# One fused linear-attention and two-MLP kernel: small first loads on SyncE's queue, late weights in one transfer each, and a new listed order

## The chip, the cores and the metric

The kernel runs on one core of one Trainium2 chip. The time is device time in microseconds (us) of one execution; the kernel before takes 922.84 us (median of three runs, 921.71 to 923.36). The engines are named as in the profile: PE is TensorE, PEld its weight loads, DVE VectorE, ACT ScalarE, POOL GpSimd, SP SyncE. SPq and ACTq mark the issue of a transfer (DMA) by SP or ACT.

## What is computed

Three stages, the output of one being the input of the next; q, k, v and the result are float32, the six weight matrices arrive as 64-bit floats. q is drawn eight times wider than k and v.

```python
def _attn_ref(q, k, v):                      # (4, 8, 576, 64) each
    q_s = softmax of q over its last axis; k_s = softmax of k over the sequence
    kv = np.einsum('bhsd,bhse->bhde', k_s, v)
    return np.einsum('bhsd,bhde->bhse', q_s, kv)
x = attention, as 2304 tokens x 512
x = (silu(x @ w_gate) * (x @ w_val)) @ w_out       # 512 -> 1536 -> 512
x = ((x @ w_a) * (x @ w_b)) @ w_out                # 512 -> 1536 -> 512
```

(The two softmaxes are written out in the reference, with 1e-9 added to each sum.)

## The kernel before, in words

**Number format.** A float32 product is made of three products in PE's fp32r format: each operand is split into a high part, rounded by a copy on ACT (L432, L542), and a low part, the rest, by a subtraction on DVE or POOL (L425 is the line of the helper that all two-operand additions and subtractions go through). The weights are read raw, as pairs of 32-bit words, and are brought to float32 by a chain of six operations on ACT, DVE and POOL (L516 to L543 for the early ones, L586 to L605 for the late ones; `a<-wr`, `early<-early` and `late<-late` in the rows).

**Attention** is cut into 16 units, one for each batch and pair of heads. The 576 rows of a head are 512 main rows, four to a partition, and a rest of 64. A unit loads k, q and v (`ut`, `ua`, `uc`, `uq`), takes the column maxima of k (`tm`, then a transposition `kx` on PE, then a reduction `kr` on DVE, L778, and a transposition back, `kb`), subtracts, exponentiates on ACT (L812 for k and q at once), multiplies k by v (`kv`, L840), scales, turns q (`qt`, `ql`) and multiplies (`xt`, `xl`). For batch 0 the rests of all four units are loaded together into one buffer `rests` by six transfers of 64 KB: two for k, two for q, two for v (`load_rests`, L622). They are issued by ACT.

**First MLP.** 1536 hidden columns are 12 blocks f. For each token tile of 512 rows and each f there are two up-products (`u`, 12 matmuls each), a gate (ACT L989, DVE L992), the split of the gated product into `h` (ACT L432, DVE L425), and four down-products into `acc`. The first two tiles run in this form. A bank of up-products comes free when `h` of the block before is written. While tile 0 runs, the kernel also converts the 12 weight blocks and does the attention of batch 1; while tile 1 runs, batches 2 and 3.

**Later.** From about 280 us on the tokens go in three groups (`SUPER`, L1162), in which the products of pairs of blocks are combined so that fewer matmuls are needed at the price of more additions (`p`, `q`, `o`, `temps`, `raww`, `l2w` in the rows). The weights of the second MLP are converted beside this, between 170 and 580 us, by `convert_late` (L561): 36 pieces of a third of a block each, 512 KB raw, into buffers `early` or `late`.

**The order.** Nothing is scheduled at run time. Every operation has a number; `ORDER` (L72) lists all 3,732 in the order in which they are handed out, and each engine works through its own in that order, waiting where an input or a buffer is not ready. `SECOND` (L42) lists the operations that run on their second possible engine (POOL in place of DVE, ACT in place of DVE, and so on), `PLACE` (L60) picks buffers, and `UNREAD` (L68) puts transpositions of the identity whose result nobody reads (`unread`, L1624) ahead of listed products, so many each. A transfer is issued by its engine in the same order, and the issue itself waits where an earlier transfer on the same semaphore has not landed (eight of them go round).

Of the kernel before, what the change touches and what calls it, by code (L numbers as in the profile page):

```python
# [30 lines left out]
class Plan:  # L31
# [27 lines left out]
    )  # L59
    PLACE = (  # L60
        "00102103011010010221301001112132030011031011101100000010001110112101000100110001111020101110001101121110"
        "00101110110021010011010001110010010101100101111110010010110100000011010001111011100101100100011111100101"
        "01010110010101000110110110100101101010101010110110111100101010000010000110110101101101001011101001101011"
        "00101001102130123020110311010102013020110311010102013020110311010102013010120311010101023021301021301010"
# [4 lines left out]
        29, 7, 31, 3, 69, 3, 101, 14, 105, 7, 43, 25, 88, 1, 141, 8, 115, 3, 151, 6, 124, 2, 128, 3, 648, 21, 255,  # L69
        1, 654, 8, 657, 17,  # L70
    )
    ORDER = (  # L72
# [270 lines left out]
def kernel(  # L343
# [24 lines left out]
    nc = tc.nc  # L368
    B, H, S, D = q.shape
    DM = H * D  # L370
    DFF = w_gate.shape[1]
    P = 128
# [12 lines left out]
    WC, WH = 512, 256  # L385
# [65 lines left out]
    mats = [[m.bitcast(U32) for m in ms] for ms in ((w_gate, w_val, w_out), (w_a, w_b, w_out2))]  # L451
# [109 lines left out]
    def convert_late(f, m):  # L561
# [3 lines left out]
        def r():  # L565
            return buf()[:, at:at + 1024].rearrange("p (h n t) -> p h n t", h=2, t=2)
# [1092 lines left out]
```

## Time and profile before

| | |
|---|---|
| median of 3 runs | 922.84 us |
| the profiled execution | 924.12 us |
| its span in the trace | 922.3 us |
| PE busy | 902.8 us (98%) |
| DVE busy | 706.6 us (77%) |
| ACT busy | 537.1 us (58%) |
| POOL busy | 400.0 us (43%) |
| granted TensorE clock, whole span | 1.00 |

The profiled execution is 1.3 us longer than the median. A span is counted from the start of the trace; 1.8 us of the 924.12 lie outside it. Busy time is the union of an engine's instructions, without the issue of transfers. A row of the timeline gives start and length in us, engine, line, operation, output and inputs, how many instructions were merged, and in brackets how long the engine sat idle before and what ended that.

### The profile page before, as it was taken

The page shows a single profiled execution, that of the slowest core. Times are in us where ns is not written, and L with a number is a line of the kernel's source. Part 1 is how long each engine was busy: PE and PEld are TensorE (multiplying, and loading weights), DVE is VectorE, ACT ScalarE, POOL GpSimd, SP SyncE. Part 2 cuts the span into 40 slices and gives each one's busy share as a digit, 9 for nine tenths or more (in the row PEclk, how much of TensorE's full clock was granted, in tenths as well). Part 3 has the DMA queues.
Part 4 walks back from the last instruction along what each step waited for, and adds up shares of the span by engine and source line. Part 5 has one row for each costly group of instructions (what it writes and reads, how often), then busy time and mean ns, then how long its engine had stood idle before and what let it go on. Part 6 is the DMA issues. An engine that isn't in the chain of part 4 may idle for free.

```text
span 922.3 us, 13897 instructions
## 1 busy us (share of the span) xinstructions
PE 902.8 (98%) x4851; PEld 757.4 (82%) x4851; DVE 706.6 (77%) x1148; ACT 537.1 (58%) x983; POOL 400.0 (43%) x380
## 2 busy tenths in 40 slices
PE   7899999999999999999999999999999999999998
PEld 6677777777787888888888888888788898988986
DVE  6999996689888698888868767547797586776845
ACT  4999976557765775655563556333544573553530
POOL 5322121344323453756356622254554343575720
PEclk9999999999999999999999999999999999999999
DMA  9888775588854323142433653212231220101003
GB/s 269 269 262 280 239 233 172 165 258 271 272 167 137 97 87 96 55 124 80 129 135 107 201 154 109 80 46 92 80 103 58 92 69 23 47 24 46 24 1 115
DMA packets 108302, 121.50 MB, mean 132 GB/s; under 512 B 31944, under 2 KB 84168, under 8 KB 108104
## 3 DMA queue, kind: packets, MB, share of 16 engines
q1 hardware_dynamic: 102568, 116.55, 40.3%
q10 hardware_dynamic: 5664, 4.07, 1.4%
q8 instruction: 38, 0.62, 0.3%
q14 instruction: 32, 0.26, 0.1%
HBM read 88.60 MB, written 31.98 MB: 131 GB/s over the span
## 4 chain that ended last, share of the span: by engine, by line
PE 73%; DVE 1%; issue 0%; DVEq 0%
PE p L1295 37%; PE o L1430 10%; PE q L1404 7%; PE u L970 2%; PE o L1432 2%; PE o L1439 2%; PE acc L1005 2%; PE o_a L1516 2%; PE o_b L1516 2%; PE o_d L1516 2%; PE o_a L1511 1%; PE o_b L1511 1%; PE o_d L1511 1%; PE o_e L1516 1%; PE o_e L1511 1%; DVE raww L425 0%
## 5 line engine op out<-in xcount | busy, mean ns | idle before, releaser
L1295 PE MATMUL p<-l2w,l2w 128*128 128x512 f32 x1512 | 360.7, 390 | 2.1 <-DVE temps L425 2.1
L1295 PEld LDWEIGHTS p<-l2w,l2w 128*128 128x128 f32 x1512 | 280.7, 188 | 59.4 <-DVE temps L425 2.9
L425 POOL TENSOR_TENSOR l2w<-raww,l2w 128x512 fp32r<-128x512 f32 x68 | 95.3, 1405 | 157.1 <-ACT l2w L432 157.0
L970 PE MATMUL u<-xhl,w 128*128 128x512 f32 x552 | 138.8, 399 | 2.6 <-DVE h L425 1.6
L432 ACT CAST l2w<-raww 128x512 fp32r<-128x512 f32 x144 | 87.8, 621 | 67.1 <-PE p L1295 23.3
L970 PEld LDWEIGHTS u<-xhl,w 128*128 128x128 f32 x552 | 100.8, 188 | 25.5 <-DVE h L425 1.9
L425 DVE TENSOR_TENSOR temps<-p,temps 128x512 f32<-128x512 f32 x90 | 61.7, 686 | 48.2 <-PE p L1295 47.6
L425 DVE TENSOR_TENSOR l2w<-raww,l2w 128x512 fp32r<-128x512 f32 x76 | 63.4, 840 | 25.4 <-ACT l2w L432 25.4
L1308 ACT COPY temps<-p 128x512 f32<-128x512 f32 x72 | 41.9, 588 | 58.1 <-PE p L1295 58.0
L1005 PE MATMUL acc<-h,w 128*128 128x512 f32 x288 | 74.6, 401 | 0.0
L1404 PE MATMUL q<-rest,l2w 128*128 128x256 f32 x432 | 65.5, 283 | 0.0
L1005 PEld LDWEIGHTS acc<-h,w 128*128 128x128 f32 x288 | 52.4, 188 | 11.9 <-issue 1.0
L425 DVE TENSOR_TENSOR sums<-o,sums 128x512 f32<-128x512 f32 (+1 forms) x65 | 44.0, 679 | 20.6 <-PE o L1430 14.8
L1404 PEld LDWEIGHTS q<-rest,l2w 128*128 128x128 f32 x432 | 58.3, 192 | 0.5
L1430 PE MATMUL o<-l2w,hp 128*128 128x512 f32 x165 | 55.5, 391 | 0.0
L425 POOL TENSOR_TENSOR raww<-raww 128x256 f32<-128x256 f32 (+1 forms) x32 | 36.6, 1144 | 41.9 <-DVE l2w L425 24.6
L1430 PE MATMUL o<-l2w,l2w 128*128 128x512 f32 x168 | 49.5, 389 | 0.0
L602 POOL TENSOR_TENSOR late<-late 128x512 uint32<-128x512 uint32 x15 | 20.8, 1384 | 51.2 <-DVE late L597 36.5
L1430 PEld LDWEIGHTS o<-l2w,l2w 128*128 128x128 f32 x168 | 31.5, 188 | 6.6
L1430 PEld LDWEIGHTS o<-l2w,hp 128*128 128x128 f32 x165 | 30.7, 188 | 6.9 <-DVE sums L425 0.4
L425 DVE TENSOR_TENSOR sums<-o_e,sums 128x512 f32<-128x512 f32 x36 | 23.8, 684 | 10.5 <-ACT sums L1535 5.0
L432 ACT CAST l2w<-temps 128x512 fp32r<-128x512 f32 x36 | 22.1, 620 | 15.9 <-PE o L1430 7.6
(264 smaller groups left out, 1793.5 us busy)
## 6 DMA issues: line engine op xcount, KB each, us to landing
raww<-wf SPq DMA_DIRECT2D x36, 512.0 KB, 3.9
raww<-wf SPq DMA_DIRECT2D x36, 256.0 KB, 3.4
wf<-a SPq DMA_DIRECT2D x16, 384.0 KB, 3.0
wr<-in_moe_w_gate_dram SPq DMA_DIRECT2D x22, 256.0 KB, 4.0
wr<-in_moe_w_val_dram SPq DMA_DIRECT2D x22, 256.0 KB, 3.7
wr<-in_moe_w_out_dram SPq DMA_DIRECT2D x22, 256.0 KB, 4.5
wf<-late SPq DMA_DIRECT2D x20, 256.0 KB, 2.4
wf<-early SPq DMA_DIRECT2D x16, 256.0 KB, 5.4
```

The lines of the kernel that those rows point to most:

```text
L425: engine.tensor_tensor(out=out(), in0=x(), in1=y(), op=op)
L432: add("scalar", act_us(n), lambda: nc.scalar.copy(out=hi(), in_=src()), src_keys, [hi_key])
L602: engine.tensor_tensor(out=u32(), in0=u32(), in1=r()[..., 0], op=ALU.add)
L970: nc.tensor.matmul(ps()[:, 0:n], lhsT=wv[:, c, :], rhs=x()[:, xs, c, 0:n], start=(a == 0 and c == 0), stop=(a == 2 and c == KD - 1))
L1005: nc.tensor.matmul(ps()[:, 0:n], lhsT=w()[:, 4 + ws, o * P:(o + 1) * P], rhs=h()[:, hs, 0:n], start=begin, stop=end)
L1295: nc.tensor.matmul(ps()[:, 0:width], lhsT=wv(o)[:, m, ws, c, :], rhs=ops_x[o][xs][1]().rearrange("p (c n) -> p c n", c=2)[:, c, 0:width], ...
L1308: add("scalar", act_us(n), lambda: nc.scalar.copy(out=to[1]()[:, 0:n], in_=ps()[:, 0:n]), [ps], to[0] if isinstance(to[0], list) else [to[ ...
L1404: nc.tensor.matmul(ps[m]()[:, 0:256], lhsT=wv(o)[:, m, ws, c % 2, :], rhs=rest_x[xs][1]().rearrange("p (c n) -> p c n", c=KD)[:, c, :], st ...
L1430: nc.tensor.matmul(ps(), lhsT=lhs(i, hs), rhs=outs_w[i][1]()[:, ws * 512:(ws + 1) * 512], **ends)
L1432: nc.tensor.matmul(ps()[:, 0:width], lhsT=outs_w[i][1]()[:, ws * 512 + r * P:ws * 512 + (r + 1) * P], rhs=hs2[i][t][1]()[:, hs * 512:hs * ...
L1511: nc.tensor.matmul(ps()[:, 0:width], lhsT=wu()[:, at:at + P], rhs=h()[:, hs * 512:hs * 512 + width], start=first and a == 0, stop=a == 2, ...
L1516: nc.tensor.matmul(ps()[:, r * 256:(r + 1) * 256], lhsT=h()[:, hs * 512 + (2 * g + r) * P:hs * 512 + (2 * g + r + 1) * P], rhs=wu()[:, ws ...
```

## The change

Three things.

1. `load_rests` issues its six transfers through SP's queue in place of ACT's. (The planner's label `queue="scalar"` stays; what is issued where is set by the call.)
2. `convert_late` loads a piece of `w_a` or `w_b` in one transfer of 512 KB, in place of two of 256 KB; 24 pieces are concerned. Pieces of `w_out` had one already.
3. `SECOND`, `PLACE`, `UNREAD` and `ORDER` are new lists for the same operations.

```diff
     UNREAD = (
-        29, 7, 31, 3, 69, 3, 101, 14, 105, 7, 43, 25, 88, 1, 141, 8, 115, 3, 151, 6, 124, 2, 128, 3, 648, 21, 255,
-        1, 654, 8, 657, 17,
+        29, 7, 31, 3, 69, 3, 101, 3, 105, 11, 43, 31, 88, 6, 141, 9, 115, 5, 124, 10, 128, 8, 648, 26, 654, 14, 657,
+        12,
     )
...
             if m < 2:
-                for h in range(2):
-                    nc.sync.dma_start(
-                        out=r()[:, h].rearrange("p (c n) t -> p c (n t)", n=P),
-                        in_=mats[1][m][h * DM // 2:(h + 1) * DM // 2, f * 2 * P:(f + 1) * 2 * P].rearrange(
-                            "(c p) n -> p c n", p=P))
+                nc.sync.dma_start(
+                    out=buf()[:, at:at + 1024].rearrange("p (c n) -> p c n", n=2 * P),
+                    in_=mats[1][m][:, f * 2 * P:(f + 1) * 2 * P].rearrange("(c p) n -> p c n", p=P))
...
         for h in range(HG):
-            dma(lambda h=h: nc.scalar.dma_start(
+            dma(lambda h=h: nc.sync.dma_start(
                 out=rests_kq()[rest(h), at, :, h, :] if at < 2 else rests_v()[rest(h)],
                 in_=src[b, :, SM:S, :].rearrange("(g h) s d -> h s g d", h=HG)[h]),
```

By instruction counts PE has 19 more of the unread transpositions (148 for 129) and is otherwise unchanged, SP has 18 transfers fewer (24 fewer late ones, six rests more), ACT six fewer issues, and some ten operations change between DVE, POOL and ACT. On PE the new order moves single attention products by a few places up to about 236 us and leaves everything after that as it was. Line numbers after L575 are two lower in the changed file.

**The first transfers.** On SP the kernel starts with these rows; `ut0` to `ut3` are the four units of batch 0, `wr0_0_0` is the first third of weight block 0. Before:

```order
L715 DMA ut0_92<-in_k_dram 128x2x256
L715 DMA ut1_94<-in_k_dram 128x2x256
L715 DMA ut0_92<-in_q_dram 128x2x256
L715 DMA ut1_94<-in_q_dram 128x2x256
L715 DMA ut2_105<-in_k_dram 128x2x256
L715 DMA ut2_105<-in_q_dram 128x2x256
L487 DMA wr0_0_0_123<-in_moe_w_gate_dram 128x4x256
L715 DMA ut3_125<-in_k_dram 128x2x256
L715 DMA ut3_125<-in_q_dram 128x2x256
L726 DMA ut0_92<-in_v_dram 128x4x64 x2
L726 DMA ut1_94<-in_v_dram 128x4x64 x2
```

In the changed kernel:

```order
L713 DMA ut0_92<-in_k_dram 128x2x256
L713 DMA ut1_94<-in_k_dram 128x2x256
L713 DMA ut0_92<-in_q_dram 128x2x256
L713 DMA ut1_94<-in_q_dram 128x2x256
L623 DMA rests_97<-in_k_dram 64x4x64 x2
L713 DMA ut2_103<-in_k_dram 128x2x256
L713 DMA ut2_103<-in_q_dram 128x2x256
L487 DMA wr0_0_0_126<-in_moe_w_gate_dram 128x4x256
L713 DMA ut3_128<-in_k_dram 128x2x256
L713 DMA ut3_128<-in_q_dram 128x2x256
L724 DMA ut0_92<-in_v_dram 128x4x64
L623 DMA rests_97<-in_q_dram 64x4x64 x2
L623 DMA rests_97<-in_v_dram 64x4x64 x2
L724 DMA ut0_92<-in_v_dram 128x4x64
```

The six transfers of `rests` now stand in SP's row: k behind the first four tiles, q and v behind the gate weights, k and q of unit 3 and half of v of unit 0.

On DVE the same stretch begins (the first three rows are alike) with `kr0`, the column maxima of unit 0; `st` holds the row maxima of q, and `st0<-rests` is the one that reads the rest of q. Before:

```order
L778 TENSOR_REDUCE kr0_136<-kx0_117 128x1
L778 TENSOR_REDUCE kr1_140<-kx1_132 128x1
L797 TENSOR_REDUCE st0_142<-ut0_92 128x8
L425 TENSOR_TENSOR ut0_92<-ut0_92,kb0_153 128x2x4x64
L800 TENSOR_REDUCE st0_142<-rests_97 128x1
L797 TENSOR_REDUCE st1_161<-ut1_94 128x8
L800 TENSOR_REDUCE st1_161<-rests_97 128x1
L425 TENSOR_TENSOR ut1_94<-rests_97,kb1_156 128x128
L425 TENSOR_TENSOR tm2_169<-ut2_105 128x2x2x64
```

In the changed kernel:

```order
L776 TENSOR_REDUCE kr0_132<-kx0_115 128x1
L776 TENSOR_REDUCE kr1_138<-kx1_130 128x1
L795 TENSOR_REDUCE st0_140<-ut0_92 128x8
L425 TENSOR_TENSOR tm2_160<-ut2_103 128x2x2x64
L795 TENSOR_REDUCE st1_162<-ut1_94 128x8
L798 TENSOR_REDUCE st0_140<-rests_97 128x1
L776 TENSOR_REDUCE kr2_173<-kx2_169 128x1
L425 TENSOR_TENSOR ut1_94<-rests_97,kb1_154 128x128
L425 TENSOR_TENSOR tm3_176<-ut3_128 128x2x2x64
L798 TENSOR_REDUCE st1_162<-rests_97 128x1
L425 TENSOR_TENSOR ut1_94<-ut1_94,kb1_154 128x2x4x64
```

The rest maxima of q of unit 0 stood behind a subtraction and ahead of unit 1's; now they stand ahead of `kr2`, `kb1`'s subtraction and all that follows. The subtraction `ut0<-ut0,kb0` has gone to POOL.

**Weight block 7 beside tile 0, f = 5.** On DVE, where `h0_0_5` is the low part of the gated product of block 5 and `a0_7_0`, `a0_7_1` are the two halves of weight block 7 in conversion. Before:

```order
L523 TENSOR_SCALAR a0_7_0_1136<-a0_7_0_1136 128x768
L526 TENSOR_SCALAR a0_7_0_1136<-a0_7_0_1136 128x768
L532 SCALAR_TENSOR_TENSOR a0_7_0_1136<-wr0_7_0_1062,a0_7_0_1136 128x768
L518 TENSOR_SCALAR a0_7_1_1170<-wr0_7_1_1111 128x768
L537 ISA a0_7_0_1136<-wr0_7_0_1062,a0_7_0_1136 128x1536
L523 TENSOR_SCALAR a0_7_1_1170<-a0_7_1_1170 128x768
L425 TENSOR_TENSOR h0_0_5_1189<-u0_0_5_1_1100,h0_0_5_1189 128x512
```

In the changed kernel:

```order
L523 TENSOR_SCALAR a0_7_0_1152<-a0_7_0_1152 128x768
L526 TENSOR_SCALAR a0_7_0_1152<-a0_7_0_1152 128x768
L425 TENSOR_TENSOR h0_0_5_1181<-u0_0_5_1_1117,h0_0_5_1181 128x512
L532 SCALAR_TENSOR_TENSOR a0_7_0_1152<-wr0_7_0_1076,a0_7_0_1152 128x768
L518 TENSOR_SCALAR a0_7_1_1185<-wr0_7_1_1128 128x768
L537 ISA a0_7_0_1152<-wr0_7_0_1076,a0_7_0_1152 128x1536
```

`h0_0_5` has moved ahead of the operation that reads the second half's raw words (`a0_7_1<-wr0_7_1`), and three others.

**The change from the second group of tokens to the third.** On DVE; `p11_0_1` and so on are banks of up-products of step 11, `raww` and `spare` hold float32 weights, `r12`, `r2a01` and `r2wr11` tokens. Before:

```order
L425 TENSOR_TENSOR temps_3136<-p11_0_1_6158,temps_3136 128x512
L425 TENSOR_TENSOR l2w2_2869<-r12_6168,l2w2_2869 128x1024
L425 TENSOR_TENSOR temps_3136<-p11_0_2_6150,temps_3136 128x512
L425 TENSOR_TENSOR r12_6168<-r12_6168,r2a01_6173 128x1024
L425 TENSOR_TENSOR r2a01_6173<-r2a01_6173,r2wr11_6175 128x1024
L425 TENSOR_TENSOR raww_2932<-raww_2932,spare_3022 128x512
L425 TENSOR_TENSOR temps_3136<-p11_1_1_6211,temps_3136 128x512
```

In the changed kernel:

```order
L425 TENSOR_TENSOR temps_3136<-p11_0_1_6150,temps_3136 128x512
L425 TENSOR_TENSOR raww_2936<-raww_2936,spare_3027 128x512
L425 TENSOR_TENSOR l2w2_2869<-r12_6160,l2w2_2869 128x1024
L425 TENSOR_TENSOR temps_3136<-p11_0_2_6142,temps_3136 128x512
L425 TENSOR_TENSOR r12_6160<-r12_6160,r2a01_6165 128x1024
L425 TENSOR_TENSOR r2a01_6165<-r2a01_6165,r2wr11_6167 128x1024
L425 TENSOR_TENSOR temps_3136<-p11_1_1_6204,temps_3136 128x512
```

The subtraction `raww<-raww,spare` has moved from right ahead of `temps<-p11_1_1,temps` to five places earlier.

## Rows read from the trace of the kernel before

**Rows 1.** Windows: stretch, its length, busy PE, PEld, DVE, ACT, POOL, clock, DMA, GB/s

```profile
0.00:51.00 51.00, 41.00 (x306) 32.83 (x307) 42.04 (x82) 37.16 (x80) 21.07 (x36) 1.00 0.89 276
51.00:110.00 59.00, 57.34 (x289) 45.35 (x290) 56.89 (x92) 56.03 (x111) 15.34 (x25) 1.00 0.82 261
110.00:220.00 110.00, 109.73 (x619) 86.58 (x619) 89.47 (x192) 75.64 (x126) 35.13 (x70) 1.00 0.70 216
220.00:238.00 18.00, 17.16 (x110) 13.05 (x111) 16.17 (x38) 11.80 (x18) 9.67 (x19) 1.00 0.80 244
238.00:904.00 666.00, 663.57 (x3471) 568.34 (x3470) 493.67 (x734) 356.13 (x651) 318.82 (x233) 1.00 0.29 92
```

**Rows 2.** Waits of PE: total us, times, longest us

```profile
PE p L1295 <- DVE temps L425: 2.1, 2, 1.3
...
PE u L970 <- DVE h L425: 1.6, 2, 0.9
...
PE kb L780 <- DVE kr L778: 0.8, 2, 0.4
```

**Rows 3.** Timeline of SP, first 18 us

```profile
3.00 0.64 SPq L715 DMA_DIRECT2D ut<-in_k_dram  x1
4.45 0.37 SPq L715 DMA_DIRECT2D ut<-in_q_dram  x1
7.16 0.37 SPq L487 DMA_DIRECT2D wr<-in_moe_w_gate_dram  x1
```

**Rows 4.** Timeline of ACT, first 12 us

```profile
0.78 1.40 ACTq L625 DMA_DIRECT2D rests<-in_k_dram  x2
2.20 1.93 ACTq L625 DMA_DIRECT2D rests<-in_q_dram  x2
...
11.15 0.65 ACTq L625 DMA_DIRECT2D rests<-in_v_dram  x1
11.84 0.27 ACT L783 COPY kb<-kb 128x128 f32<-128x128 f32 x1 [3.15 <-PE unread L1624]
```

**Rows 5.** Timeline of DVE, 3 to 13 us

```profile
3.53 0.43 DVE L425 TENSOR_TENSOR tm<-ut 128x256 f32<-128x256 f32 x1 [3.53 <-DMA ut<-in_k_dram]
...
9.75 0.28 DVE L800 TENSOR_REDUCE st<-rests 128x1 f32<-128x128 f32 x1
...
10.54 0.27 DVE L800 TENSOR_REDUCE st<-rests 128x1 f32<-128x128 f32 x1
12.14 0.53 DVE L425 TENSOR_TENSOR ut<-rests,kb 128x128 f32<-128x128 f32 x1 [1.32 <-ACT kb L783]
12.60 0.41 DVE L425 TENSOR_TENSOR tm<-ut 128x256 f32<-128x256 f32 x1
```

**Rows 6.** Windows of the first loads and of the first block

```profile
8.00:13.00 5.00, 3.45 (x19) 2.97 (x19) 3.67 (x9) 1.42 (x3) 3.79 (x8) 1.00 1.03 307
12.14:50.80 38.66, 33.15 (x270) 26.64 (x270) 37.27 (x70) 35.11 (x77) 16.08 (x23) 1.00 0.91 283
```

**Rows 7.** DVE by line and form to 60 us: count, busy us, mean ns

```profile
L851 DVE TENSOR_SCALAR ut<-kv,ks 64x64 f32<-64x64 f32 x2 | 0.6, 278 | 0.0
```

**Rows 8.** Timeline of DVE, 96 to 99 us

```profile
96.33 0.56 DVE L518 TENSOR_SCALAR a<-wr 128x768 uint32<-128x768 uint32 x1 [0.81 <-DMA wr<-in_moe_w_out_dram]
...
98.15 0.68 DVE L425 TENSOR_TENSOR h<-u,h 128x512 fp32r<-128x512 f32 x1
```

**Rows 9.** Timeline of DVE, 663 to 665.5 us

```profile
663.24 1.78 DVE L425 TENSOR_TENSOR raww<-raww,spare 128x512 f32<-128x512 f32 x1
664.94 0.68 DVE L425 TENSOR_TENSOR temps<-p,temps 128x512 f32<-128x512 f32 x1
```

**Rows 10.** Timeline of PE, 39 to 42 us

```profile
39.81 2.45 PE L1624 MATMUL unread<-ident 128*128 128x128 f32 x21
```

**Rows 11.** Issues of late weights: KB each, median us to landing

```profile
late<-in_moe_w_b_dram SPq DMA_DIRECT2D x14, 256.0 KB, 2.7
late<-in_moe_w_out_dram SPq DMA_DIRECT2D x7, 512.0 KB, 3.8
```

More of the change, by code (lines that the diff above doesn't have):

```diff
@@ L55 @@
         3194, 3195, 3198, 3210, 3212, 3267, 3286, 3288, 3290, 3292, 3299, 3308, 3313, 3314, 3316, 3318, 3326, 3330,
[3 rows of a table removed]
[3 rows of a table added]
     )
     PLACE = (
[L61 to L64, printed above, removed]
+        "00102103011000110221101013120123011300103011001100001000110101121011001000110011011021001110100011121110"
+        "10010110110021010101001100110010010011100110111110010010110010000011010001011111100101100101100111101001"
+        "01100101100110000110101110010101101010101010110110111010101000010100000110110101101011001011100101110011"
+        "00101001110230123020110311010102013020110311010102013020110311010102013010120311010101023021301021301010"
         "10101010123010101012301010101012301010101012301010101012301010101012301010101010123010123010102011031101"
@@ L584, in convert_late @@
         A1, LOW, HIGH = [(buf, (at, x)) for x in range(3)]
-        dma(get, P * 2 * WH * 8, [], [LOW, HIGH], issue=0.95 if m < 2 else 0.37, after=first)
+        dma(get, P * 2 * WH * 8, [], [LOW, HIGH], issue=0.55 if m < 2 else 0.37, after=first)
         add("scalar", act_us(2 * WH) + 0.08, lambda: nc.scalar.activation(
```

418 rows, old and new, of tables (ORDER, SECOND) are left out of this document.

## The prediction

> **What bounds the kernel now.** I read the busy times by stage first, then TensorE's waits, then the timelines of the stretches in which it waits. The windows show that TensorE is the bound: it idles 51.0 - 41.0 = 10.0 us in the first 51 us, 59.0 - 57.34 = 1.7 us from 51 to 110, 0.3 us to 220, 18.0 - 17.16 = 0.8 us to 238, and 666.0 - 663.57 = 2.4 us from there to 904, at a granted clock of 1.00, the 2.4 GHz level, throughout [rows 1]. Its matmuls are the same in both kernels, but for the unread ones. So the change can move the time in two ways only: by when the first block of the first MLP gets going, and by the 5.2 us of idle pieces behind 51 us.
>
> In the first 51 us the pace is VectorE's. From 12.14 us to 50.8 us, where the first low part `h` is written, it is busy 37.27 of 38.66 us [rows 6]; `h` frees the bank for the next up-product. So what counts there is when VectorE can start its unbroken run, and how much it must do before `h`. In the kernel before, the run starts at 12.14 us, after 1.32 us of idling for a copy of `kb` on ScalarE [rows 5]. The bracket of that copy names TensorE, but ScalarE issued a transfer of `rests` from 11.15 to 11.80 and copied at 11.84 [rows 4]: the copy stood behind an issue, and the issue behind an earlier landing.
>
> **Part 1: the rests on SyncE's queue.** ScalarE loses six issues; the four for k and q take 1.40 + 1.93 us, the last 0.65 us [rows 4]. In the first 12 us it has nothing else urgent but the copies of `kb`, so the gain is the end of the wait of 1.32 us, and something else is late next. In the new order VectorE reads the q rests of unit 0 ahead of `kr2` and of all that follows. They are now the 13th and 14th transfer in one queue. Up to them the queue holds eight tiles of 256 KB, two k rests of 64 KB, the gate weights of 512 KB, one transfer of v of 128 KB, and they themselves are 128 KB: 2944 KB. The first 256 KB are there at 3.53 us [rows 5]. The other 2688 KB, 2.75 MB, go at the 307 GB/s of the stretch from 8 to 13 us [rows 6] in 9.0 us: the q rests land at about 12.5 us. That is 0.4 us later than the start at 12.14 us, and before them VectorE can only do what it also did before 12.14.
>
> What VectorE must do from there to `h` differs little: two more reductions of q rests (0.28 and 0.27 us [rows 5]) and one more scaling (0.28 us [rows 7]), one maximum `tm` less (0.41 us [rows 5]): +0.4 us. The first `h` therefore comes at 12.5 + 38.7 + 0.4 = 51.6 us in place of 50.8: **+0.8 us**. The bounds: VectorE had run out of work at 10.8 us [rows 5], so an earlier landing can give back at most 1.3 us, and with the 0.4 us added the gain ends at 0.9 us. At the other end, SyncE held twice in the kernel before, from 3.64 to 4.45 us and from 4.82 to 7.16 us [rows 3], 3.15 us in which it issued nothing although the next transfer had no input to wait for; if the rests come to stand behind such holds the start slips by as much, to +3.95 us. I take the value of the byte count, because it rests on the rate of the very stretch.
>
> The kernel before shows the q rests early: SyncE issued tiles from 0.74 us on, the q rests were issued by ScalarE until 4.13 us [rows 4], and VectorE read those of unit 0 at 9.75 us without idling [rows 5], so they had landed 2.75 us or more ahead of my 12.5. The Trainium skill ("DMA: Bandwidth & Descriptors", section "Queues, rings and completion order") states that each transfer engine goes round between the queues that have work, packet by packet. By that rule a short load in a queue of its own overtakes a long one, and moving it gives the place away; the trace agrees as far as the 9.75 goes. It speaks against this part, and it is why the slower rival below has weight.
>
> **Part 2: one transfer for a late piece.** 24 pieces lose one issue each on SyncE. The two halves of 256 KB landed 2.7 us after issue, a transfer of 512 KB 3.8 us [rows 11]; even if each piece came 1.1 us later, it is converted far ahead of its use, from 170 to 580 us, and no row of TensorE's waits names it. I put it at 0. If that cover were gone, 24 x 1.1 us would be off VectorE's and ScalarE's slack, not off TensorE; at worst one wait of 1.1 us, and at best a wait of ScalarE's or VectorE's on them goes, which TensorE does not see.
>
> **Part 3: the order behind 51 us.** Three places can be read off.
> - At 96 us VectorE idled 0.81 us for a landing of weights in L518, and `h` of block 5 came behind it at 98.15 [rows 8]; TensorE waited 0.88 us for it, the longer of its two waits on `h` (rounded 0.9 there) [rows 2]. In the new order `h` stands ahead of that read. **-0.9 us**; at worst 0, if `h` now waits for its high part on ScalarE.
> - At 663.24 us a subtraction of 1.78 us stood ahead of `temps` at 664.94 [rows 9], for which TensorE waited 1.3 us [rows 2]. It has moved five places forward. **-1.3 us**; at worst 0.
> - One of TensorE's two waits for `kr`, 0.4 us, is on a unit of batch 3 [rows 2]. The product of it, `kb14`, stood behind three down-products and now stands behind nine. **-0.4 us**.
>
> Against this a new order makes new waits. In the kernel before, the 2.4 us from 238 to 904 [rows 1] fall on three or four places of some 0.3 to 1.3 us each, so one new wait is about **+0.5 us** (none, or three: 0 to 1.5).
>
> The unread transpositions go from 129 to 148. A run of 21 takes 2.45 us [rows 10], 0.117 us each, so 19 more are 2.2 us of TensorE, all listed ahead of the second block's products. They fill time in which it waits for VectorE, which runs without a gap; I count 0, and +2.2 us where that cover is gone.
>
> **The sum.** +0.8 - 0.9 - 1.3 - 0.4 + 0.5 = -1.3 us, against the profiled execution's 924.12 us: 922.8. That execution lies 1.28 us above the median of the runs shown, and the same steps from 922.84 give **921.5 us**.
>
> **The rivals.**
> - *The start gains too.* If the q rests land when VectorE runs out of work, the first term is -0.9 in place of +0.8, the sum -3.0: 919.8 us. For it: SyncE's hold of 2.34 us [rows 3] ended with the landings of transfers that shared the engines with ScalarE's queue. Against it: 2.75 MB in 7.3 us would be 378 GB/s, and the rows show 307.
> - *The rests come too late: slower.* One queue holds them behind 2.8 MB, and each hold of SyncE's shifts them. With the two holds of the kernel before in front of them they land at 12.5 + 3.15 = 15.65 us, and the sum is -1.3 + 3.15 = +1.9: 924.7 us. Nothing is gained from a landing at 13.8 us on; the loss can be told from about 15.6 us on, and grows by 1 us for each. The skill's rule above leads here. Against it: with the loads in the order of need there are fewer landings to hold for.
> - *The waits move, and nothing comes of it.* VectorE is busy 56.89 of 59 us from 51 to 110 and ScalarE 56.03 [rows 1]. If what is saved at 98 us is waited for at the next block, and the rest of the gains is lost likewise, the sum is +0.8 - 0.4 = +0.4: 923.2 us. Against it: from 110 to 220 us TensorE idles 0.3 us in 110, so there is slack again behind.
>
> **How the numbers follow.** Forecast 0.45, start gains too 0.27, rests too late 0.17, nothing comes of it 0.11. A measurement of this kernel can tell about 0.2%, 1.85 us, from no change, so faster means under 921.0. The forecast's own range is 919.8 to 922.9 (its terms at half their bounds); it lies mostly within 0.2%: 0.12 of its 0.45 is faster, 0.33 the same. The first rival adds 0.27 to faster and the slower rival 0.16 to slower (0.01 same); the last one is 0.08 same, 0.02 slower and 0.01 faster. Together 0.40 faster, 0.42 the same, 0.18 slower. The range reaches down to 917.8 (the first rival's 919.8, less 2 of the 2.6 us that are then left of the idle pieces) and up to 925.0 (just above the slower rival's 924.7); about 2 in 10 lies outside.
>
> **What would show it.** Right: VectorE's first read of the q rests waits for a landing, at 12 to 13 us, and the copies of `kb` on ScalarE follow the transpositions at once; the first `h` ends at 51 to 52 us; no wait of TensorE's near 98 us and none on `temps` near 664. Wrong: the q rests read at under 11.5 or over 14 us; `h` moved by another amount than the landing; the waits on `h` and on `temps` still among TensorE's, or new ones above 1 us behind 110 us, above all on converted late weights.

## The result, and the profile after

The changed kernel takes 928.05 us (median of 6 runs), the kernel before 923.10 beside it: a ratio of 1.0056, with a 95% interval of 1.0042 to 1.0071. It is slower by 5 us. The forecast was 921.5, its range ended at 925.0, and the sign was wrong. The profiled execution of the changed kernel took 927.93 us (span 925.9). Of all executions here one, of e6, took 2319 us; its ratio leaves it out.

The stages of the kernel after, as windows, with the columns of [rows 1]:

```profile
0.00:51.00 51.00, 40.63 (x303) 32.79 (x304) 40.47 (x77) 32.99 (x64) 22.60 (x37) 1.00 0.84 250
51.00:110.00 59.00, 57.76 (x294) 44.84 (x293) 57.53 (x91) 55.43 (x120) 13.75 (x22) 1.00 0.83 268
...
238.00:904.00 666.00, 662.97 (x3475) 567.61 (x3474) 491.38 (x739) 355.78 (x651) 320.33 (x238) 1.00 0.30 94
```

TensorE's busy time is about that of before in each stage. That hides the loss: 19 more unread transpositions count as busy, and the first up-product started at 30.7 us before and at 36.6 after. Between the two profiles the same work stands 3.1 us later at the first `h`, 4.0 at the second block's first up-product (45.2 us before), 5.5 from 250 to 650 us, 3.9 just behind 664 us, where the profile before has a wait that this one has not, and 3.6 at the end. The granted clock is 1.00, the 2.4 GHz level, as before. TensorE's waits in the kernel after, which answer to [rows 2]:

```profile
PE qt L889 <- POOL ut L872: 2.8, 2, 2.5
PE kx L773 <- DMA rests<-in_k_dram: 2.4, 1, 2.4
PE kx L773 <- DVE km L425: 2.0, 1, 2.0
...
PE u L968 <- ACT s L987: 0.8, 1, 0.8
PE p L1293 <- DVE temps L425: 0.8, 1, 0.8
```

The waits on `h` and the 1.3 us on `temps` are gone. In their place stand one at the start on `qt`, a longer one on the k rests (2.4 us, before 1.5) and one of 2.0 us on `km` (the column maxima of k, in the last unit), which begins at 238.6 us. SyncE's issues of the rests in the kernel after, which answer to those of ScalarE in [rows 4]:

```profile
2.76 1.41 SPq L623 DMA_DIRECT2D rests<-in_k_dram  x2
7.58 1.39 SPq L623 DMA_DIRECT2D rests<-in_q_dram  x2
```

ScalarE's copies of `kb` come as soon as TensorE has them, as forecast:

```profile
9.66 0.27 ACT L781 COPY kb<-kb 128x128 f32<-128x128 f32 x1 [7.64 <-PE kb L778]
11.21 0.27 ACT L781 COPY kb<-kb 128x128 f32<-128x128 f32 x1 [1.29 <-PE kb L778]
```

And VectorE's timeline, which answers to [rows 5], with the first `h` as its last row:

```profile
8.20 0.42 DVE L425 TENSOR_TENSOR tm<-ut 128x256 f32<-128x256 f32 x1 [3.98 <-PE kx L773]
...
13.58 0.28 DVE L798 TENSOR_REDUCE st<-rests 128x1 f32<-128x128 f32 x1 [1.37 <-DMA rests<-in_q_dram]
...
14.45 1.28 DVE L425 TENSOR_TENSOR tm<-ut 128x256 f32<-128x256 f32 x1
...
16.45 0.91 DVE L518 TENSOR_SCALAR a<-wr 128x512 uint32<-128x512 uint32 x1
17.39 1.51 DVE L523 TENSOR_SCALAR a<-a 128x512 f32<-128x512 f32 x1
...
20.99 1.63 DVE L532 SCALAR_TENSOR_TENSOR a<-wr,a 128x512 uint32<-128x512 uint32 x1
...
53.27 0.68 DVE L425 TENSOR_TENSOR h<-u,h 128x512 fp32r<-128x512 f32 x1
```

The reader is to see three things. VectorE idles 3.98 us at 4.2 us for the chain that begins with the k rests, and 1.37 us for the q rests, which it reads at 13.58 and not at 9.75. Then it runs without a gap, but four instructions take 1.28, 0.91, 1.51 and 1.63 us, which in the profile before took 0.42, 0.42, 0.42 and 1.02. The first `h` ends at 53.94 us, 3.1 us later than in the profile before. GpSimd's timeline has what lies beside the long ones:

```profile
14.34 1.10 POOL L802 TENSOR_TENSOR ut<-ut,st 128x512 f32<-128x512 f32 x1
16.00 0.78 POOL L806 TENSOR_TENSOR ut<-rests,st 128x128 f32<-128x128 f32 x1 [0.56 <-DVE st L798]
...
17.04 1.45 POOL L425 TENSOR_TENSOR ut<-ut,kb 128x512 f32<-128x512 f32 x1
...
20.82 1.26 POOL L872 TENSOR_TENSOR ut<-ut,st 128x640 f32<-128x640 f32 x1 [2.20 <-DVE st L869]
```

Each of the four long ones was started while one of these ran, and ended 0.3 to 0.6 us after it: 15.73 against 15.44, 17.36 against 16.78, 18.90 against 18.49, 22.62 against 22.08.

### The profile page after: what moved, and what is told of

Same layout as the page of the kernel before. It is cut to its first block, busy times and chain, and to the rows that moved or that the text cites. A ratio compares the mean times of both kernels' runs of the same rounds, so it can differ in the third digit from the quotient of the medians.

```text
span 925.9 us, 13846 instructions
## 1 busy us (share of the span) xinstructions
PE 906.0 (98%) x4870; PEld 760.0 (82%) x4870; DVE 705.6 (76%) x1149; ACT 534.7 (58%) x981; POOL 398.9 (43%) x381
## 4 chain that ended last, share of the span: by engine, by line
PE 87%; DVE 4%; DMA 3%; ACT 2%; issue 2%; POOL 1%; SPq 1%; ACTq 0%; DVEq 0%; POOLq 0%
PE p L1293 37%; PE u L968 11%; PE o L1428 10%; PE q L1402 7%; PE acc L1003 6%; PE o L1430 2%; PE o L1437 2%; PE o_d L1514 2%; PE o_a L1514 1%; PE o_b L1514 1%; PE o_a L1509 1%; PE o_b L1509 1%; PE o_d L1509 1%; PE kv L838 1%; PE xt L902 1%
## 5 line engine op out<-in xcount | busy, mean ns | idle before, releaser
L425 DVE TENSOR_TENSOR l2w<-raww,l2w 128x512 fp32r<-128x512 f32 x75 | 60.6, 814 | 24.2 <-ACT l2w L432 24.1
L425 POOL TENSOR_TENSOR raww<-raww 128x256 f32<-128x256 f32 (+1 forms) x31 | 34.3, 1105 | 45.7 <-DVE l2w L425 30.2
L425 DVE TENSOR_TENSOR raww<-raww 128x512 f32<-128x512 f32 (+1 forms) x41 | 32.6, 794 | 5.5 <-POOL l2w L425 3.6
```

Source lines behind the costliest of these rows:

```text
L425: engine.tensor_tensor(out=out(), in0=x(), in1=y(), op=op)
```

## The experiments

In the lists below the numbers are operations: 2 and 3 are the k rests, 5 and 6 the q rests, 8 and 9 the v rests. All ratios are to the kernel before, run on the same chip; each row is of 5 to 12 runs. Of a list that an edit changes, only the places that change are shown.

| kernel | median us | ratio | 95% interval |
|---|---|---|---|
| the changed kernel | 928.05 | 1.0056 | 1.0042 to 1.0071 |
| e10: the changed kernel again | 927.47 | 1.0054 | 1.0038 to 1.0069 |
| e4: changed, old unread list | 927.15 | 1.0040 | 1.0027 to 1.0054 |
| e1: changed, rests on ScalarE's queue | 924.59 | 1.0018 | 1.0008 to 1.0029 |
| e5: changed, all rests early on SyncE's | 924.48 | 1.0020 | 1.0010 to 1.0030 |
| e16: changed, q rests early | 925.61 | 1.0018 | 1.0003 to 1.0033 |
| e6: e1, a product back on VectorE | 925.95 | 1.0035 | 1.0023 to 1.0047 |
| e8: e5, a product back on VectorE | 925.45 | 1.0029 | 1.0018 to 1.0040 |
| e7: new order alone | 925.54 | 1.0031 | 1.0019 to 1.0043 |
| e15: new order alone, again | 924.43 | 1.0009 | 0.9997 to 1.0021 |
| e14: new order to 54 us, then old | 924.28 | 1.0003 | 0.9988 to 1.0017 |
| e13: old order to 54 us, then new | 923.41 | 0.9998 | 0.9985 to 1.0011 |
| e9: the kernel before again | 922.88 | 1.0004 | 0.9994 to 1.0013 |
| e2: before, rests on SyncE's queue | 924.67 | 1.0011 | 1.0000 to 1.0021 |
| e3: before, single late pieces | 924.78 | 1.0016 | 1.0005 to 1.0028 |
| e11: before, v rests issued later | 923.19 | 1.0013 | 1.0002 to 1.0025 |
| e12: before, rests early on SyncE's | 923.89 | 1.0023 | 1.0013 to 1.0033 |

**The rests: which queue, and where in it.** Theory: the rests come late, and the start waits for them. Rival: the new order's work at the start is longer, whatever the queue. The first run gives the rests back to ScalarE:

```diff
-            dma(lambda h=h: nc.sync.dma_start(
+            dma(lambda h=h: nc.scalar.dma_start(
```

> The changed kernel with its new order and single late transfers, but with the six loads of the rests issued by ScalarE again. The traces of the two kernels show the start as the loss: the first low part h ends at 53.94 us after the change and at 50.80 before it, and VectorE's first read of the q rests comes at 13.58 us (waiting for a landing) in place of 9.75. Queue theory: the new order needs the rests when they land late, so the old queue brings the read back to 9.5 to 10.5 us, the first h to about 51, and the time to 924.5 to 925.5 us (3 us gained of the 5). Order theory: the run of VectorE that follows is what became longer, whatever the queue: the read comes early, h still ends at 53 to 54, and the time stays at 927 to 928.5.

The second leaves them on SyncE and moves them forward in the list; the third moves the q rests alone (`2, 3, 5, 6, 11`):

```diff
-        1, 4, 7, 0, 10, 2, 3, 11, 28, 29,
+        1, 4, 2, 3, 7, 0, 10, 5, 6, 11, 28, 29,
...
-        16, 5, 6, 34,
+        16, 34,
```

> The changed kernel, but in SyncE's queue the two k rests stand behind the first two k tiles (3rd and 4th, not 5th and 6th) and the two q rests behind the first two q tiles (7th and 8th, not 13th and 14th); all else is the changed kernel. In the run with the new order and the old queue everything of VectorE's from 7 to 52 us came 2.3 to 2.5 us earlier, and h ended at 51.67 us and not at 53.94. Landing theory (what counts is when the rests are there, not which queue brings them): the k rests land at about 5.5 us, the q rests at about 7, the read of the q rests does not wait, the first h ends at 50.5 to 51.7 us, and the time is 923.5 to 925. Queue theory (SyncE's queue itself is slower, through its holds or because the tiles behind come later): h stays at 53 to 54 us, the time at 927 to 928.5. A rival to both: the loads put back by it (the third and fourth tiles, the gate weights) become the late ones, h at 52 to 53, 925.5 to 927.

> The changed kernel, with the two q rests moved up to stand behind the k rests, 7th and 8th in SyncE's queue; the k rests stay 5th and 6th, behind four tiles. In the changed kernel VectorE idled 3.98 and 3.75 us at 4.2 us (two profiles; 2.9 with the old queue, 1.74 with both early), a chain that begins with the k rests, and 1.37 and 2.38 us for the q rests. If the q rests alone are the 3.3 us: as with both early, h at 51.3 to 51.8, 924.5. If the k rests matter as well, by the 1.1 us by which they land later than with the old queue: h at 52 to 52.8, 925.2 to 926.2.

VectorE's read of the q rests and its first `h` in the first of them:

```profile
11.04 0.27 DVE L798 TENSOR_REDUCE st<-rests 128x1 f32<-128x128 f32 x1
...
51.00 0.69 DVE L425 TENSOR_TENSOR h<-u,h 128x512 fp32r<-128x512 f32 x1
```

in the second:

```profile
10.97 0.27 DVE L798 TENSOR_REDUCE st<-rests 128x1 f32<-128x128 f32 x1
...
50.64 0.69 DVE L425 TENSOR_TENSOR h<-u,h 128x512 fp32r<-128x512 f32 x1
```

and in the third:

```profile
11.86 0.27 DVE L798 TENSOR_REDUCE st<-rests 128x1 f32<-128x128 f32 x1
...
51.92 0.69 DVE L425 TENSOR_TENSOR h<-u,h 128x512 fp32r<-128x512 f32 x1
```

None of the three reads waits, the first `h` comes 1.3 to 2.6 us earlier than in the kernel after's first profile (0.8 to 2.1 than in its second), and the ratios fall from 1.0056 and 1.0054 to 1.0018 to 1.0020. Of the 5 us, 0.0036 x 923 = 3.3 us are the place of the rests, shown by either queue (by the intervals 2 to 4.5, an estimate). That SyncE's queue is slower in itself falls: at an early place in it the time is that of ScalarE's. The ratios do not tell the k rests from the q rests: the third run has the chain of the k rests as late as the kernel after (3.75 us of idling), its `h` 0.9 and 1.3 us later than the others', as expected if the k rests matter, and the same ratio.

**The two programs once more.** Nothing is edited.

> The kernel before itself, unchanged, for how far apart two sets of executions of one program come out, and for a second profile of it. Two other kernels with its order had neither the wait of 0.88 us at 98 us nor the 1.29 us on temps at 664 us in full: with the rests on SyncE's queue they were 0.51 and 0, with single late pieces 0.14 and 0. Theory that these two waits belong to the order: both are there again, at 0.8 to 0.9 and 1.3 us. Theory that they belong to one execution, made by landings that vary: at least one is gone or below half its size. The ratio to the kernel before is 1.000 within 0.001; if it is 1.0015, differences of that size between kernels say nothing.

> The changed kernel itself, unchanged, beside the kernel before on this chip, and a second profile of it. If the start and the queue are the cause, whatever the execution: time ratio 1.0045 to 1.006, first h at 53 to 54.5 us. The wait of 1.98 us for km at 238.6 us was 1.91, 0.24, 0.42, 0.45, 0.49 and 1.59 us in the other runs with the new order: if it goes with the rests in SyncE's queue behind the large tiles it is 1.9 to 2.0 again, if it varies with the execution it can be anything from 0.2 to 2.0.

The kernel before is 1.0004 of itself, so a difference of 0.1% between sets says little. The changed kernel's 1.0054 agrees with its 1.0056, and its second profile again reads the q rests late:

```profile
14.30 0.29 DVE L798 TENSOR_REDUCE st<-rests 128x1 f32<-128x128 f32 x1 [2.38 <-DMA rests<-in_q_dram]
```

The waits moved. In the second profile of the kernel before TensorE waited 0.58 us on `h` at 99.75 us, and not at all on `temps` near 664; the copy of `kb` came later than in the first:

```profile
12.81 0.29 DVE L425 TENSOR_TENSOR ut<-rests,kb 128x128 f32<-128x128 f32 x1 [2.37 <-ACT kb L783]
...
97.78 0.56 DVE L518 TENSOR_SCALAR a<-wr 128x768 uint32<-128x768 uint32 x1 [0.55 <-DMA wr<-in_moe_w_out_dram]
```

Its first `h` ended at 52.49 us, against 50.82 in the first profile, and this execution is still 1.5 us shorter (922.65 against 924.12). Part of the late `h` is TensorE's clock. TensorE had idled 2.11 us up to 13.49 us; from 14.0 to 17.5 us its granted clock was 0.51, the 1.2 GHz level, and a run of 25 unread transpositions took 3.91 us, where it took 2.95 in the first profile:

```profile
13.49 0.33 PE L775 MATMUL kx<-ident,tm 128*128 128x128 f32 x1 [2.11 <-DVE tm L425]
...
15.46 3.91 PE L1624 MATMUL unread<-ident 128*128 128x128 f32 x25
```

Such a stretch stands in the profiles of e12 (0.50 from 19.4 to 22.6 us, after 1.52 us of idling) and e13 (0.51 from 12.8 to 16.2 us, after 1.91 us) too, and in e16's at 218 to 222 us (0.50, after a wait of 1.97 us on `kb`; this execution took 930.25 us, the set's median is 925.61). None of the eleven profiles with the new start has one in its first 51 us, though TensorE idled 2.50 us for `qt` in the kernel after. The mean granted clock of an execution goes with its time: of the executions of the kernel before, 25 with 0.997 or less took 923.97 us in the mean, 64 with 0.999 or more took 922.36.

In the second profile of the changed kernel the wait on `km` is 0.23 us and not 1.98, and a wait of 1.70 us stands at 97.84. The expectation that these waits belong to one execution held in full for those at 664 and 238.6 us; of the one at 98 us two thirds were there again.

Why the one at 664 comes and goes, VectorE's and GpSimd's timelines tell. GpSimd's row in the first profile of the kernel before, beside the subtraction of [rows 9] that started at 663.24 and took 1.78 us:

```profile
662.58 1.89 POOL L425 TENSOR_TENSOR l2w<-raww,l2w 128x512 fp32r<-128x512 f32 x1 [3.13 <-ACT l2w L432]
```

The same two in the second profile, VectorE's first:

```profile
663.30 0.68 DVE L425 TENSOR_TENSOR raww<-raww,spare 128x512 f32<-128x512 f32 x1
663.60 1.55 POOL L425 TENSOR_TENSOR l2w<-raww,l2w 128x512 fp32r<-128x512 f32 x1 [3.13 <-ACT l2w L432]
```

And in e11, which has this order as well:

```profile
664.45 1.34 POOL L425 TENSOR_TENSOR l2w<-raww,l2w 128x512 fp32r<-128x512 f32 x1 [3.13 <-ACT l2w L432]
664.55 1.78 DVE L425 TENSOR_TENSOR raww<-raww,spare 128x512 f32<-128x512 f32 x1
```

Where VectorE is first its subtraction takes 0.68 us and TensorE does not wait; where GpSimd is first by 0.10 or 0.66 us it takes 1.78 and TensorE waits 0.75 or 1.29 us. The four other profiles with this order there (e2, e3, e12, e14) have VectorE first by 0.02 to 0.29 us, a subtraction of 0.68 or 0.69 us, and no wait of TensorE's.

**What the order costs.** Every kernel so far with the new order and early rests kept some 1.7 us or more over the kernel before. The new order with neither other edit was run twice, and the two orders were spliced: the first 330 operations of one list (with their engines, buffers and unread transpositions), then what is left in the order of the other.

> The new order with neither of the two other edits: rests on ScalarE's queue, late pieces in two halves. The run with the new order, the old queue and single late pieces was 1.0018 of the kernel before, the one with the old order and single late pieces 1.0016. If the single pieces cost these 1.5 us wherever they stand, the order alone is 923.1 to 923.4. If they cost nothing, and those runs differ by the variation from one execution to the next, the order alone is 924.6 like its fellow, and the order is what costs 1.5 us.

> The new order alone once more, for how firm its 1.0031 is (the kernel before against itself gave 1.0004, with an interval of 0.001 to either side). If the order costs 1.5 to 2.5 us: 1.0016 to 1.0031 again. If the first set was chance: 1.000 to 1.001.

> The two orders spliced, with the queue and the halved late pieces of the kernel before: the first 330 operations of the list (to about 54 us, behind the first down-products) in the old order, with its engines and unread transpositions, all that follow in the new one. The new order alone was 1.0031 of the kernel before. If the order costs its 1.5 to 2.5 us in the first 54 us, this kernel has none of it: 922 to 923. If it costs them behind, at the waits that all runs of the new order show (0.65 us on kb at 110, 0.2 to 2.0 on km at 236), it is 924.5 to 925.5. If the spread between executions is all there is, 923 to 924.5 and no difference from its counterpart.

> The counterpart: the first 330 operations in the new order, all that follow in the old one; the queue and the halved late pieces of the kernel before. If the start costs it, 924.5 to 925.5; if what follows does, 922.5 to 923.5.

1.0031 the first time and 1.0009 the second; the splices 0.9998 and 1.0003. By these the order alone costs 2.9 us, or 0.8, and none of these runs places it. The four edits of the old order (e2, e3, e11, e12) lie at 1.0011 to 1.0023, as high as the new order's kernels with early rests, so a cost of the order itself is not shown. e13 was the candidate to beat both kernels; it equals the one before. The profile of e15 shows what an execution adds by itself. It took 927.92 us, the set's median is 924.43, and among its waits of TensorE stand, from 60 to 110 us and from 600 to 700 us:

```profile
PE xt L904 <- issue: 1.7, 1, 1.7
...
PE p L1295 <- DVE temps L425: 1.4, 1, 1.4
```

e7, the same program, has neither in its profile; e10 has the first.

**The old order with the new queue.** Three variants of the kernel before: the queue alone, as in the changed line above; the rests early on SyncE's queue (the list as in e5); and, with ScalarE's queue, the v rests behind the first two copies of `kb`.

```diff
-        16, 9, 34, 8, 70, 17,
+        16, 34, 70, 8, 9, 17,
```

> The kernel before with its old order and its halved late transfers, but with the six loads of the rests on SyncE's queue, where the old order lists them: behind the first four tiles, so the rests are 5th to 8th in the queue and not 13th and 14th. Queue theory: it is the place in the queue that counts, and here the place is early: 1.3 MB at the 307 GB/s of the early stretch puts the q rests at about 7 us, ScalarE copies kb without the issue in front, VectorE idles less than the 1.32 us at 12 us, and the time is 922 to 923.3 us. Order theory: the queue is nothing, 923.1 as before. A rival that neither has: the rests now stand ahead of the later tiles, which land 0.8 us later each; then the start slips by 0.5 to 1 us, 923.6 to 924.1.

> The kernel before with its old order and halved late pieces, but the rests on SyncE's queue at the early places: k rests 3rd and 4th, q rests 7th and 8th. With the new order these places gave 924.48 us, against 928 behind the large tiles. If the landing is all that counts, the k rests land at 5.2 us in place of 6.68, the q rests at 8.7, VectorE's idle pieces of 2.14 and 1.32 us shrink by 1 to 2 us in sum, the first h ends at 49 to 50.3 us, the time is 921 to 922.5. If the order costs as much as the landing, this kernel is 2 us faster than its fellow with the new order, 922.5. Rival: the gate weights and the third and fourth tiles, which come later here, are waited for (0.71 and 0.32 us in the run with the old order and the rests 5th to 8th), h at 51 to 52, 923.5 to 924.5.

> The kernel before with one edit: ScalarE issues the two v rests behind its copies of kb of units 0 and 1, and not one ahead of each. In the kernel before VectorE idled 1.32 us at 10.82 us for the copy that stood behind the issue of 11.15 to 11.80. If that reading is right and nothing else is late there, the copy comes at 10.5 to 10.9 us, VectorE's run starts 1.0 to 1.3 us earlier, the first h ends at 49.5 to 50 us, and the time is 921.5 to 922.3, faster than both kernels. Rival: the next input (the third k tile, the gate weights) is late by as much, h at 50.5 to 51, no change in time.

All three are the same as the kernel before or up to 0.2% slower, so no theory's gain came. In e12 the k rests were there and VectorE's idling at 5.2 us fell from 2.14 to 0.45 us, but it then idled 0.83 us for the gate weights, whose L518 took 1.90 us, and the first `h` ended at 50.69 us; the time is the rival's (its profile is also one of those in which the granted clock fell). In e11 the copy stood behind no issue, and VectorE took the product at 10.38 us without the wait of 1.32 us of [rows 5]. It idled further on for TensorE:

```profile
18.40 0.16 DVE L844 TENSOR_SCALAR ks<-kv 128x1 f32<-128x1 f32 x1 [1.53 <-PE kv L840]
```

The cause of the first wait was read rightly. The next one is in part the edit's own: both v rests are issued at 10.69 us (before, one at 4.17 and one at 11.15), ScalarE's copy of them stands for their landing, and the last four products of the first `kv` for that copy:

```profile
17.43 0.54 ACT L760 COPY ut<-rests 128x64 f32<-128x64 f32 x3 [2.14 <-DMA rests<-in_v_dram]
...
18.02 0.34 PE L840 MATMUL kv<-ut 128*64 128x65 f32 x4 [1.11 <-ACT ut L760]
```

The sixteen products ahead of them began at 16.23 us, 1.1 us earlier than those of the kernel before. So what the end of the first wait is worth by itself, e11 does not show.

**Single pieces, and the unread transpositions.**

> The kernel before with its old order and ScalarE's issue of the rests; only the late weight pieces are one transfer each. Both theories: nothing, 923.1 us within 0.7, since no wait of TensorE's names a late piece before or after. Rival: a piece that comes 1.1 us later delays its conversion and with it one of the stages behind 110 us, +1 us or more.

> The changed kernel with the table of unread transpositions of the kernel before: 129 in place of 148, otherwise the same. If the 19 more stand on TensorE's path, 2.2 us come back at 0.117 us each: 925.8 us. If they only fill time in which it waits, 928 us as after the change, and where a run of 31 (3.60 us, ahead of the first kv product at 18.23 us) is now 25, 0.7 us at most: 927.3.

e3 alone is 1.0016; but with the new order the single pieces (e1, 1.0018) are not above the halved ones (1.0031 and 1.0009). No cost of theirs is shown, and no wait of TensorE's in its profile names a late piece. e4 came out between its two expectations, and its interval reaches into that of the changed kernel: not settled. Its profile reads the q rests at 15.00 us, after 3.09 us of waiting, and ends the first `h` at 54.13 us.

**VectorE's long instructions.** In e6 and e8 the first subtraction of `kb`, operation 35, is VectorE's again:

```diff
     SECOND = (
-        35, 36, 46, 47,
+        36, 46, 47,
```

> The new order with the rests on ScalarE's queue, and one operation moved between engines: the first subtraction of kb from the keys of unit 0 (128x512) is done by VectorE, as in the kernel before, and not by GpSimd (1.26 us there, 0.82 on VectorE before). Up to the first h VectorE has the same 82 instructions before and after the change, but their durations add up to 47.93 us before and 49.71 after, although this one left it: tm at 14.4 us takes 1.28 in place of 0.42, L518 0.91 in place of 0.42, L523 1.51 in place of 0.83, L532 1.63 in place of 1.02, all while GpSimd works. Theory of the stretched instructions: GpSimd's work, put back by 1.26 us, now lies beside these; with it off GpSimd the stretches shrink by 1.5 to 2.5 us, VectorE gains 0.7 to 1.7 us net of the 0.82, the first h ends at 50 to 51 us in place of 51.67, the time falls by 0.7 to 1.7 from the 924.6 of the run without this edit. Rival: the stretches come from other work of GpSimd's that lies where it lay, VectorE has 0.82 us more to do, h at 52.5, 925.4.

> The changed kernel with both edits of its start: the rests early in SyncE's queue, and the first subtraction of kb on VectorE. If the landing and the stretched instructions are separate causes, the gains add: the first h ends at 49.5 to 51 us, the time is 922 to 924 us, at or below the kernel before. If they are one (an early landing already moves GpSimd's work out of the way), it is the time of the run with the early rests alone, within 0.7 us.

The theory fell. In e6 L518, L523 and L532 took 0.91, 1.51 and 1.63 us once more, a subtraction of 0.37 us became one of 1.01, the first `h` ended at 52.85 us, and the time was 925.95: the rival's. In e8 the gains did not add: `tm` at 10.10 us took 1.28 us beside GpSimd's L802 (9.73 us, 1.37 long). That the two meet again wherever VectorE starts is argued from such rows, not tested.

## Why the prediction was wrong

**Part 1, the start: the wrong step was the sum from the landing to `h`, in both terms.** The q rests were put at 12.5 us; they were read on landing at 13.58 and 14.30. The byte count was right in kind. Its rate was too high: 2688 KB from 3.53 us [rows 5] to the read at 13.58 is 2.75 MB in 10.05 us, 274 GB/s, where I took the 307 of five good microseconds [rows 6] (the second profile: 10.88 us, 253 GB/s). From the read to `h` I counted 38.7 + 0.4 = 39.1 us; it was 40.36 and 39.1. The +0.4 counted instructions at their usual length; four of them took 3.1 us more in the first profile (5.33 against 2.28), part of which the run gave back by idling 0.7 us in place of 1.4. In the second profile L518 and L523 took 0.62 and 0.53 us, not 0.91 and 1.51, which is the 1.26 us between 40.36 and 39.1. So the first `h` came at 53.94 and 53.42, and not at 51.6: +3.1 and +2.6 us in place of +0.8. The row on which I chose was there: VectorE had read the q rests at 9.75 us without idling, and the new order read them at 11.0 us without a wait (e1, e5). A later read is paid for the most part: reads 2.5, 3.3 and 4.0 us later than e1's (13.58, 14.30, and 15.00 in e4) put the first `h` 2.3, 1.7 and 2.4 us later. The sum had no term for the k rests either: TensorE's wait on them grew from 1.47 to 2.42 us, and VectorE's idling before the second `tm` to 3.98. By e16 that is 0.9 to 1.3 us of the first `h` in the profiles, and nothing in the ratios.

**Part 2** had no row against it: 0, within what the runs can tell (e3).

**Part 3: the gains at 98 and 664 us were events of one execution.** I took -0.9 and -1.3 us from the profiled execution. In six profiles of kernels with the old order throughout the wait at 98 us was 0.88, 0.58, 0.51, 0.14, 0.83 and 0.43 us, a mean of 0.56, the one at 664 was 1.29, 0.75 and four times none, a mean of 0.34. The new order has their like in some executions (1.70 at 97.84 in e10, on `xt` and with no releaser shown; 1.43 at 668 in e15), 0.37 and 0.13 us in the mean of its eleven profiles. By these means the two gains are 0.4 us and not 2.2. That I then took the gain from the median as well was the plain error: the profiled execution lay 1.28 us above it, and these two waits may well have been in that excess (the second profile, with 0.58 and 0 us there, took 922.65). The -0.4 at `kb14` came, and a wait of 0.65 us on another `kb` at 112.7 us came with it; a wait of 0.75 to 0.79 us on `s` near 108 us, in all seven profiles with the old order there, went as well. The new wait, +0.5, was 1.98 us in the first profile, for a late landing of a q tile of batch 3:

```profile
238.70 0.69 DVE L795 TENSOR_REDUCE st<-ua 128x8 f32<-128x512 f32 x1 [1.64 <-DMA ua<-in_q_dram]
```

In the ten other profiles with the new order behind 54 us it was 0.2 to 0.5 seven times and 1.1 to 1.9 three times; the mean of the eleven is 0.83, so the +0.5 was low by a little. The unread transpositions at 0 are neither confirmed nor refuted (e4). For the 1.7 of the 5 us that stay when the rests are early, no step is shown, and the cause is open.

**The rivals.** *The rests come too late* is what happened, and its chance of 0.17 was too small. Its 924.7 us was still 3.4 too low, because its sum kept the gains of part 3. Its mechanism was off in one point: SyncE made no holds in front of the q rests, it issued from 0.74 to 8.97 us without a gap of note. The bytes in front of them were enough. The rule of the Trainium skill that I set beside it ("DMA: Bandwidth & Descriptors", section "Queues, rings and completion order") led to the right side. The runs agree as far as a place in one's own queue is an early place; e5 shows that an early place in the shared queue does as well. *The start gains too* failed on the landing.

## What to carry to other kernels

When small loads move into a queue of large ones, count the bytes in front of each at a rate that holds over the whole stretch, and set the landing against the time at which its reader could first use it; here the place was worth about 3.3 us and the queue itself nothing. A wait read from one profile is a gain only if it is in other executions: compare the profiled time with the median first, take a second profile, and look at the granted clock stretch by stretch. Ending a wait at the start of a chain of equals (`rests`, `kb`, `kv`) is worth what the next of them leaves.

## What the runs showed of the hardware

A subtraction of VectorE's, or one of its L518, L523 and L532, with all inputs in SBUF was held when it started while one of GpSimd's ran on tensors in SBUF, until that one was done: the same 128x512 subtraction took 0.68 us when it was first by 0.30 us and 1.78 us when it came second by 0.10 us, and the four long ones at the start took 3.1 us more than in the profile before. VectorE's reduction of 640 elements (L861) was not lengthened beside GpSimd's product, nor a 128x512 subtraction that reads one of its two inputs from PSUM. The rows of the kernel after:

```profile
30.43 0.81 DVE L861 TENSOR_REDUCE st<-ut 128x10 f32<-128x640 f32 x1
34.39 0.67 DVE L425 TENSOR_TENSOR xhl<-xt,xhl 128x512 fp32r<-128x512 f32 x1
```

beside

```profile
30.06 1.57 POOL L872 TENSOR_TENSOR ut<-ut,st 128x640 f32<-128x640 f32 x1 [2.05 <-DVE st L869]
33.24 1.84 POOL L872 TENSOR_TENSOR ut<-ut,st 128x640 f32<-128x640 f32 x1 [1.47 <-DVE st L869]
```

The Trainium skill says so of VectorE's instructions with two inputs in SBUF, and of those in a mode that uses two ports ("SBUF — State Buffer", section "SBUF: two separate sides": VectorE and GpSimd share a pair of ports, and the first to start has it for the whole instruction). The trace agrees, and shows how a race decides a wait: 0.4 us in the order of two starts (e9, e11) made 0.75 us of TensorE's waiting.

The kernel before ended its first `h` at 50.82 us in one profile and at 52.49 in the other, and ran from 920.6 to 927.0 us on these chips. Part of that spread is TensorE's granted clock, which fell to 0.51 from 14.0 to 17.5 us in the second profile, after 2.11 us without work. The spread of one program is as wide as the effect of most edits here.
